# Block-transposed tiles sent from SBUF to SBUF in four transfers, in place of a way through DRAM

## The chip, the core and the metric

The kernel runs on one core of a Trainium2 chip. What counts is the time of one execution in microseconds (us) on the device. Five engines work side by side: PE multiplies matrices (PEld is its load of the stationary matrix), DVE, ACT and POOL work element by element, SP issues DMA transfers (ACT issues the stores). Each engine takes its instructions in the order of the program. On-chip data lies in SBUF, 128 partitions with a row each; PE writes to PSUM. A **stationary** operand of PE is loaded first (128 columns), the **moving** operand then streams past it, here 512 columns in a matmul.

## The reference

Queries of 4 batches, 8 heads, 768 positions and 64 features go in chunks of 32 positions. Each chunk sees 64 keys: 8 of a memory, 16 positions on the left, its own 32, and 8 on the right. The result goes through a mixture layer with two matrix products:

```python
scores = scale * np.matmul(q_c, k_full.transpose(0, 1, 3, 2))
scores = scores - np.max(scores, axis=-1, keepdims=True)
a = np.exp(scores)
a = a / (np.sum(a, axis=-1, keepdims=True) + 1e-09)
out[:, :, c_start:c_end] = np.matmul(a, v_full)
...
h = x @ w_in                                   # (3072, 512) @ (512, 1024)
e = np.exp(h - h_max)
sm = e / (np.sum(e, axis=-1, keepdims=True) + 1e-09)
solu = h * sm
ln = (solu - mu) / np.sqrt(var + 1e-06) * g_ln
return (ln @ w_out).astype(np.float32)         # (3072, 1024) @ (1024, 512)
```

## The kernel before

The 3072 rows are 24 tiles of 128. Attention works on **items**: items 0 and 1 are one tile each, items 2 to 12 two tiles each (item i holds tiles 2i-2 and 2i-1). The second part works on tiles 0 to 23. One text, ORDER, lists every step by name, in the order in which all engines get their instructions; it was planned ahead and is the same in both kernels. A name is a step and its item or tile, with the engine behind an @ (V is DVE, S is ACT, G is POOL).

For an item i the steps are: loads Lq, Lk, Lv (line 232); S, the scores on PE (line 347); M, the row maximum, and Bm, the subtraction of it (DVE, lines 370 and 377); X, the exponential (ACT, line 383); Z, the row sum (DVE, line 387); a transposition of the probabilities p; V, their product with the values (PE, line 415); N, the division by the row sum (DVE, line 429); a transposition of the result x; XH and XL, which split x into a rounded part and a rest (lines 216 or 214, and 219). For a tile t: G, 24 matmuls with w_in (line 480); Hm, He, Hu, C, Sq, Dn, the normalization; a transposition of u; UH and UL, the split; O, 24 matmuls with w_out (line 540); Os and St, the scaled store. Each of the two products is three matmuls in place of one, high by high, high by low, low by high.

A transposition is made in one of two ways. **On PE** (PT, XT, UT, line 333): items 0 to 3 and tiles 0 to 3. **By blocks** (Pt, Xt, Ut with Pw, Xw, Uw and Pr, Xr, Ur): the other 9 items, twice each (p and x), and the other 20 tiles, 38 tiles of data of 128 by 1024 in all. There DVE transposes each block of 32 by 32 in place (`square`, line 304), one transfer writes the tile to DRAM (`write`, line 312), and four transfers read it back into the same tile, each into 32 partitions (`read`, line 320):

```python
a = away[name, i].rearrange("(q n) (d e) -> q n d e", q=4, d=4)
for d in range(4):
    nc.sync.dma_start(t[SQ * d:SQ * d + SQ], a[:, :, d].rearrange("q n e -> n q e"))
```

All of these are issued by SP, in the place in ORDER of Pw and Pr (or Xw, Xr, Uw, Ur), between the loads of q, k and v. SP waits at a `read` until its `write` has landed, and what stands behind it on SP waits too. Transfers of SP and ACT count on eight semaphores in turn, so each also waits for the one eight places before it.

Tiles come from pools of buffers: `take` gives the buffer that has been free longest, and `used` gives one back after its last use.

Of the kernel before, what the change touches and what calls it, by code (L numbers as in the profile page):

```python
# [11 lines left out]
F32 = mybir.dt.float32  # L12
# [3 lines left out]
ALU = mybir.AluOpType  # L16
AX = mybir.AxisListType

P = 128
CHUNK, LEFT, RIGHT = 32, 16, 8  # L20
NEG = -1.0e30
SQ = 32
SLOTS, HALVES, RAWS, ROUNDED = 7, 6, 4, 8
SINGLES = 2
SPLIT = {0: 2}


# [2 lines left out]
ORDER = """  # L30
# [59 lines left out]
def chunked_attention_then_solu_kernel(  # L90
# [22 lines left out]
    nc = tc.nc  # L113
    D = P // 2
    NP_ = w_in.shape[0] // (2 * D)
    NT = out.shape[0] // P
    NCH = P // CHUNK
    LINE = kw.shape[0] // (NT * P * NP_)
    KEYS = P // 2
    DM, DF = w_in.shape  # L120
    items = [(t, 1) for t in range(SINGLES)] + [(t, 2) for t in range(SINGLES, NT, 2)]
    NC_ = DM // P
    NF = DF // P
    HALF = DF // 2
    TPB = 6
# [7 lines left out]
    dram = ctx.enter_context(tc.tile_pool(name="away", bufs=1, space=bass.MemoryType.DRAM))  # L133
# [5 lines left out]
    held = {}  # L139
    away = {}  # L140
# [12 lines left out]
    def get(*key):  # L153
        return held[key][0]

    def used(*key):
        held[key][1] -= 1
        if held[key][1] == 0:
            buf, _, kind = held.pop(key)
            if kind == "raw":  # L160
                rest[0] -= 1
                if rest[0] < RAWS:
                    free["slot"].extend([buf[:, 0:W], buf[:, W:2 * W]])
                    return
            free[kind].append(buf)
# [13 lines left out]
    w_in_h = const.tile([P, NC_, DF], F32R, name="w_in_h")  # L179
    w_in_l = const.tile([P, NC_, DF], F32R, name="w_in_l")  # L180
# [66 lines left out]
    def cut(ap, i, x):  # L247
        n = ap.shape[1] // SPLIT.get(i, 1)
        return ap[:, x * n:(x + 1) * n]
# [46 lines left out]
    def home(i):  # L296
        return "slot" if items[i][1] == 2 else "half"

    def square(name, item, uses):
        def step(i):  # L300
            src = get(name, i)
            kind = home(i) if item else "slot"
            t = take(kind, (name + "t", i), uses).rearrange("p (d m n) -> p d m n", d=4, n=SQ)
            nc.vector.transpose(t, src.rearrange("p (m d n) -> p d m n", d=4, n=SQ))  # L304
            used(name, i)
        return step

    def write(name):
        def step(i):
            t = get(name + "t", i)  # L310
            away[name, i] = dram.tile(list(t.shape), F32, name=f"{name}_away{i}")
            nc.sync.dma_start(away[name, i], t)
        return step

    def read(name):
        def step(i):
            t = get(name + "t", i).rearrange("p (q e) -> p q e", q=4)
            a = away[name, i].rearrange("(q n) (d e) -> q n d e", q=4, d=4)
            for d in range(4):
                nc.sync.dma_start(t[SQ * d:SQ * d + SQ], a[:, :, d].rearrange("q n e -> n q e"))  # L320
        return step

    def by_block(ap):
# [2 lines left out]
    def on_pe(name):  # L326
        def step(i):
            src = get(name, i)
            kind = "two" if name == "u" or items[i][1] == 2 else "one"
            t = take(kind, (name + "T", i), 1 if name == "p" else 2)  # L330
            t = flat(t) if kind == "two" else t
            for n in range(src.shape[1] // P):
                nc.tensor.transpose(t[:, n * P:(n + 1) * P], src[:, n * P:(n + 1) * P], ident)  # L333
            used(name, i)
        return step
# [20 lines left out]
    def by_head(i):  # L356
        n = items[i][1]
        return get("s", i)[:, :, 0:n * HALF // 2].rearrange("p r (n k) -> p r n k", k=KEYS)

    def row_max(i):  # L360
# [9 lines left out]
        nc.vector.tensor_reduce(nmax, s, axis=AX.X, op=ALU.max, negate=True)  # L370
        used("s", i)

    def below_max(i):
        n = items[i][1]
        nmax = get("nmax", i)[:, 0:2 * n * NP_].rearrange("p (r n) -> p r n", r=2).unsqueeze(3)
        a = take(home(i), ("p", i), 2).rearrange("p (n r k) -> p r n k", r=2, k=KEYS)
        nc.vector.tensor_tensor(a, by_head(i), nmax.broadcast_to([P, 2, n * NP_, KEYS]), ALU.add)
        used("s", i)
        used("nmax", i)

# [3 lines left out]

    def row_sum(i):
        s = take("per_head", ("rinv", i), 1)[:, 0:2 * items[i][1] * NP_]
        nc.vector.tensor_reduce(  # L387
            s, get("p", i).rearrange("p (n k) -> p n k", k=KEYS), axis=AX.X, op=ALU.add
        )
        nc.vector.tensor_scalar(s, s, 1e-9, None, ALU.add)  # L390
        nc.vector.reciprocal(s, s)
        used("p", i)
# [31 lines left out]
    def norm(i):  # L424
        n = items[i][1]
        rinv = get("rinv", i)[:, 0:2 * n * NP_].rearrange("p (n r) -> p r n", r=2).unsqueeze(3)
        x = take(home(i), ("x", i), 1).rearrange("p (n r d) -> p r n d", r=2, d=D)
        xp = get("xp", i)[:, :, 0:n * HALF // 2].rearrange("p r (n k) -> p r n k", k=D)
        nc.vector.tensor_tensor(x, xp, rinv.broadcast_to([P, 2, n * NP_, D]), ALU.mult)
        used("xp", i)  # L430
        used("rinv", i)

# [21 lines left out]
    def high(name, uses):  # L454
        def step(i, on):
            key, src = source(name, i)
            copy(on, target(name + "h", i, uses), src)
            used(*key)
        return step
# [9 lines left out]
    def hidden(t, c, half):  # L469
        if c == 0 and half == 0:  # L470
            take("two", ("h", t), 2)
        u, odd = divmod(t, 2)
        h = get("h", t)
        x = [
            get(n, u).rearrange("p (t c n) -> p t c n", t=2, n=P)[:, odd, c]
            for n in ("xh", "xl")
        ]
        w = (w_in_h, w_in_l)
        for i, (a, b) in enumerate(((0, 0), (0, 1), (1, 0))):
            nc.tensor.matmul(  # L480
                h[:, half], x[a], w[b][:, c, half * HALF:(half + 1) * HALF],
                start=c == 0 and i == 0, stop=c == NC_ - 1 and i == 2,
            )
        if c == NC_ - 1 and half == 1:
            used("xh", u)
            used("xl", u)
# [65 lines left out]
    def store(t):  # L552
# [24 lines left out]
def _layout(q, k, v, mem_k, mem_v):  # L577
    import numpy as np

    B, H, S, D = q.shape  # L580
    M = mem_k.shape[2]
    NPAIR = H // 2
    NCH = S // CHUNK
    KEYS = M + LEFT + CHUNK + RIGHT
    TPB = S // P
    CPT = P // CHUNK
    NT = B * TPB

    qT = q.reshape(B, NPAIR, 2, TPB, P, D).transpose(0, 3, 2, 5, 1, 4)
    qT = qT.reshape(NT, 2 * D, NPAIR, P)  # L590

    def padded(x):
        z = np.zeros((B, H, LEFT, D), x.dtype)
        return np.concatenate([z, x, z[:, :, :RIGHT]], 2)

    kp, vp = padded(k), padded(v)

    lines = []
    for t in range(TPB):
        x = kp[:, :, t * P:t * P + P + LEFT + RIGHT]  # L600
        mid = P - CHUNK
        lines.append(np.concatenate([x[:, :, :CHUNK], mem_k, x[:, :, CHUNK:mid], mem_k, x[:, :, mid:]], 2))
    kw = np.stack(lines, 1).reshape(B, TPB, NPAIR, 2, -1, D).transpose(0, 1, 3, 5, 2, 4)
    kw = kw.reshape(NT, 2 * D, NPAIR, -1)

    wins = []
    for c in range(NCH):
        x = vp[:, :, c * CHUNK:c * CHUNK + KEYS - M]
        e = 0 if c % 2 else CHUNK
        wins.append(np.concatenate([x[:, :, :e], mem_v, x[:, :, e:]], 2))  # L610
    vw = np.stack(wins, 2).reshape(B, NPAIR, 2, TPB, CPT, KEYS, D).transpose(0, 3, 2, 5, 1, 4, 6)
    vw = vw.reshape(NT, 2 * KEYS, NPAIR, CPT, D)
    def by_item(x):
        n = x.shape[0]
        late = x[SINGLES:].reshape((n - SINGLES) // 2, 2, P, -1).transpose(0, 2, 1, 3)
        return np.concatenate([x[:SINGLES].ravel(), late.ravel()])

    return by_item(qT), by_item(kw), by_item(vw)
# [28 lines left out]
```

## Time and profile before

| | |
|---|---|
| time, median of 3 runs (lowest to highest) | 359.84 us (356.36 to 359.94) |
| profiled execution: its time, its span | 359.48 us, 357.7 us |
| busy share of PE, DVE, POOL, ACT | 91%, 61%, 39%, 36% |
| mean granted clock of PE | 0.97 |
| chain that ended last, by engine | PE 61%, DMA 18%, DVE 12%, SP's queue 3%, ACT 3% |
| bytes moved by DMA | 82.31 MB, 230 GB/s on average |
| read from DRAM, written to DRAM | 55.45 MB, 26.21 MB |

The span runs from the first instruction to the last; all stretches below are counted in us from its start. "Busy" of PE is modelled, as matmuls overlap; how far apart they start says more. [...] The chain follows the last instruction back to what released it, step by step. A wait is put down to what ended it.

### The profile page before, as it was taken

The numbers are of one execution on the slowest core, as the hardware profiler recorded it, in microseconds if no ns is written. First come the engines' busy times: TensorE is split into PE (matmuls) and PEld (weight loads), VectorE is DVE, ScalarE is ACT, GpSimd is POOL, SyncE is SP. The second block draws the span as 40 slices with busy tenths as digits, with TensorE's granted clock in tenths as the row PEclk, the third lists the DMA queues.
The fourth block names the chain that finished last, engine by engine and source line by source line (L and its number), as shares of the span: only waits on it lengthen the run. The fifth ranks groups of instructions, "written<-read, shape, count | busy, mean of one in ns | idle before, by whom it ended". The sixth has DMA issues, their size and how long they took to land.

```text
span 357.7 us, 9973 instructions
## 1 busy us (share of the span) xinstructions
PE 325.8 (91%) x4324; PEld 263.7 (74%) x4324; DVE 219.7 (61%) x264; ACT 130.0 (36%) x189; POOL 138.9 (39%) x173
## 2 busy tenths in 40 slices
PE   1569999999997999979999899999959999999995
PEld 1557887888785877857887678888647888888884
DVE  1589999968966964756955386564466654037300
ACT  3256375542422414122322334422225064232521
POOL 0226061442318263752500834220523746625160
PEclk9969999999998999998999999999969999999999
DMA  7999925576897876689959679866651547435621
GB/s 296 420 422 400 405 78 199 198 252 192 302 306 218 245 267 214 220 233 353 268 191 263 194 216 382 286 188 188 212 210 60 184 114 226 128 129 173 226 90 59
DMA packets 37771, 82.31 MB, mean 230 GB/s; under 512 B 4320, under 2 KB 23776, under 8 KB 35296
## 3 DMA queue, kind: packets, MB, share of 16 engines
q1 hardware_dynamic: 34272, 75.39, 62.8%
q10 hardware_dynamic: 3456, 6.29, 4.7%
q8 instruction: 34, 0.56, 0.6%
q14 instruction: 9, 0.07, 0.1%
HBM read 55.45 MB, written 26.21 MB: 228 GB/s over the span
## 4 chain that ended last, share of the span: by engine, by line
PE 61%; DMA 18%; DVE 12%; SPq 3%; ACT 3%; issue 2%; POOL 1%; DVEq 0%; POOLq 0%; ACTq 0%
PE one L540 28%; PE two L480 23%; DMA out<-half 5%; PE two L347 4%; PE two L415 3%; SPq L320 3%; DMA q<-in_qT 2%; DMA raw<-p_away 2%; DMA k<-in_kw 2%; DVE per_head L387 2%; DMA p_away<-raw 2%; DMA raw<-x_away 1%; DMA slot<-x_away 1%; PE two L203 1%; PE two L333 1%
## 5 line engine op out<-in xcount | busy, mean ns | idle before, releaser
L480 PE MATMUL two<-w_in_h,fr 128*128 128x512 f32 x384 | 143.0, 405 | 6.8 <-DVE fr L219 4.6
L540 PE MATMUL one<-w_out_h,fr 128*128 128x512 f32 x384 | 138.1, 396 | 0.1
L480 PEld LDWEIGHTS two<-w_in_h,fr 128*128 128x128 f32 x384 | 73.4, 192 | 26.1 <-DVE fr L219 5.4
L540 PEld LDWEIGHTS one<-w_out_h,fr 128*128 128x128 f32 x384 | 72.7, 189 | 16.8 <-DVE fr L219 0.5
L480 PE MATMUL two<-w_in_l,fr 128*128 128x512 f32 x192 | 76.2, 397 | 0.2 <-DVE w_in_l L219 0.2
L540 PE MATMUL one<-w_out_l,fr 128*128 128x512 f32 x192 | 75.2, 391 | 0.0
L489 DVE TENSOR_REDUCE per_row<-two 128x1 f32<-128x1024 f32 x24 | 29.1, 1212 | 28.9 <-PE two L480 28.8
L548 ACT ACTIVATE half<-one,per_row 128x512 f32<-128x512 f32 x24 | 16.5, 687 | 82.2 <-PE one L540 80.8
L480 PEld LDWEIGHTS two<-w_in_l,fr 128*128 128x128 f32 x192 | 36.9, 192 | 7.7 <-DVE w_in_l L219 0.6
L540 PEld LDWEIGHTS one<-w_out_l,fr 128*128 128x128 f32 x192 | 36.5, 190 | 7.3
L219 POOL TENSOR_TENSOR fr<-raw,fr 128x1024 fp32r<-128x1024 f32 x13 | 31.2, 2403 | 17.4 <-ACT fr L214 16.6
L347 PE MATMUL two<-k,q 64*32 64x64 f32 x1536 | 19.6, 237 | 14.5 <-DMA k<-in_kw 7.6
L347 PEld LDWEIGHTS two<-k,q 64*32 64x32 f32 x1536 | 17.1, 111 | 18.8 <-issue 17.9
L216 POOL TENSOR_SCALAR fr<-raw 128x1024 fp32r<-128x1024 f32 x11 | 11.6, 1051 | 47.1 <-DVE slot L304 18.1
L219 POOL TENSOR_TENSOR fr<-slot,fr 128x1024 fp32r<-128x1024 f32 x9 | 21.5, 2391 | 18.1 <-DMA slot<-u_away 10.7
L494 ACT ACTIVATE slot<-two,per_row 128x1024 f32<-128x1024 f32 x12 | 13.4, 1118 | 30.6 <-DVE per_row L489 30.6
L494 ACT ACTIVATE raw<-two,per_row 128x1024 f32<-128x1024 f32 x12 | 13.4, 1115 | 27.7 <-DVE per_row L489 21.4
L216 POOL TENSOR_SCALAR fr<-slot 128x1024 fp32r<-128x1024 f32 x8 | 8.4, 1052 | 32.4 <-DMA slot<-u_away 15.3
L504 DVE CUSTOM_DVE_ANT_0 slot<-two,slot 128x1024 f32<-128x1024 f32 x12 | 14.7, 1222 | 8.1 <-ACT slot L494 8.1
L504 DVE CUSTOM_DVE_ANT_0 raw<-two,raw 128x1024 f32<-128x1024 f32 x12 | 14.5, 1206 | 7.7 <-ACT raw L494 6.2
L370 DVE TENSOR_REDUCE per_head<-two 128x16 f32<-128x1024 f32 (+1 forms) x13 | 14.8, 1135 | 5.0 <-PE two L347 4.7
L304 DVE STREAM_TRANSPOSE raw<-slot 128x1024 f32<-128x1024 f32 x10 | 12.4, 1238 | 8.1 <-POOL slot L516 5.9
(88 smaller groups left out, 372.9 us busy)
## 6 DMA issues: line engine op xcount, KB each, us to landing
v<-in_vw SPq DMA_DIRECT2D x11, 1024.0 KB, 8.5
k<-in_kw SPq DMA_DIRECT2D x11, 672.0 KB, 6.8
out<-half ACTq DMA_DIRECT2D x24, 256.0 KB, 3.0
u_away<-raw SPq DMA_DIRECT2D x12, 512.0 KB, 3.5
raw<-u_away SPq DMA_DIRECT2D x48, 128.0 KB, 3.4
q<-in_qT SPq DMA_DIRECT2D x11, 512.0 KB, 7.8
raw<-in_w_in SPq DMA_DIRECT2D x4, 1024.0 KB, 11.3
raw<-in_w_out SPq DMA_DIRECT2D x4, 1024.0 KB, 9.2
```

What stands on the lines that cost most here:

```text
L216: nc.gpsimd.tensor_scalar(out, in_, 1.0, 0.0, ALU.mult, ALU.add)
L219: (nc.gpsimd if on == "G" else nc.vector).tensor_tensor(out, a, b, ALU.subtract)
L304: nc.vector.transpose(t, src.rearrange("p (m d n) -> p d m n", d=4, n=SQ))
L320: nc.sync.dma_start(t[SQ * d:SQ * d + SQ], a[:, :, d].rearrange("q n e -> n q e"))
L347: nc.tensor.matmul(s[32 * j:32 * j + 32, r, t, g], q[rows, o + t, g, 32 * j:32 * j + 32], k[rows, o + t, g, START[j]:START[j] + KEYS], sta ...
L370: nc.vector.tensor_reduce(nmax, s, axis=AX.X, op=ALU.max, negate=True)
L480: nc.tensor.matmul(h[:, half], x[a], w[b][:, c, half * HALF:(half + 1) * HALF], start=c == 0 and i == 0, stop=c == NC_ - 1 and i == 2,)
L489: nc.vector.tensor_reduce(take("per_row", ("hm", t), 1), flat(get("h", t)), axis=AX.X, op=ALU.max, negate=True)
L494: nc.scalar.activation(take("slot", ("u", t), 2), flat(get("h", t)), AF.Exp, bias=get("hm", t), scale=1.0, accum_out=take("per_row", ("esu ...
L504: nc.vector.tensor_tensor_reduce(u, flat(get("h", t)), u, 1.0, 0.0, ALU.mult, ALU.add, accum_out=usum)
L540: nc.tensor.matmul(get("o", t), u[a], w[b][:, f], start=f == 0 and i == 0, stop=f == NF - 1 and i == 2)
L548: nc.scalar.mul(take("half", ("osb", t), 1), get("o", t), get("rstd", t))
```

## The change

The step `write` now takes a second buffer and sends the tile into it directly, in four transfers, each from 32 source partitions to all 128; `read` does nothing. By this the data land in another order: feature n of block d comes to partition 4n+d, where it was 32d+n. Everything that is multiplied with such a tile has to be in the same order. The host permutes rows and columns of w_in, and the values of tiles 6 and later. Items whose p goes by blocks get their p written by DVE in groups of 16 (`below_max`), two instructions in place of one, and their row sum is taken in two instructions. Items whose x goes through PE (0 to 3) get x written in the new order in `norm`, two instructions with a step of 4 elements. Tiles 0 to 3, whose u goes through PE, need the hidden columns in the old order: their G matmuls read w_in with a step of 32 elements (128 bytes).

```diff
@@ def write(name)
         def step(i):
-            t = get(name + "t", i)
-            away[name, i] = dram.tile(list(t.shape), F32, name=f"{name}_away{i}")
-            nc.sync.dma_start(away[name, i], t)
+            src = get(name + "t", i)
+            kind = home(i) if name != "u" else "slot"
+            uses = held[name + "t", i][1]
+            held[name + "s", i] = held.pop((name + "t", i))
+            t = take(kind, (name + "t", i), uses)
+            held[name + "s", i][1] = 1
+            src = src if len(src.shape) == 2 else flat(src)
+            e = src.shape[1] // 4
+            for q in (0, 2, 1, 3):
+                nc.sync.dma_start(t[:, e * q:e * q + e], src[SQ * q:SQ * q + SQ])
+            used(name + "s", i)
@@ def read(name)
-            t = get(name + "t", i).rearrange("p (q e) -> p q e", q=4)
-            a = away[name, i].rearrange("(q n) (d e) -> q n d e", q=4, d=4)
-            for d in range(4):
-                nc.sync.dma_start(t[SQ * d:SQ * d + SQ], a[:, :, d].rearrange("q n e -> n q e"))
+            pass
@@ def below_max(i)
+        a = take(home(i), ("p", i), 2)
+        if f"PT{i}" in todo:
...
+        else:
+            a = a.rearrange("p (n d r m) -> p r n d m", d=4, r=2, m=KEYS // 4)
+            for r in range(2):
+                nc.vector.tensor_tensor(
+                    a[:, r], by_head(i)[:, r].rearrange("p n (d m) -> p n d m", d=4),
+                    nmax[:, r].unsqueeze(3).broadcast_to([P, n * NP_, 4, KEYS // 4]), ALU.add,
+                )
@@ def row_sum(i)
+            a = get("p", i).rearrange("p (n d r m) -> p r n d m", d=4, r=2, m=KEYS // 4)
+            for r in range(2):
+                nc.vector.tensor_reduce(
+                    s.rearrange("p (n r) -> p r n", r=2)[:, r], a[:, r], axis=AX.XY, op=ALU.add
+                )
@@ def norm(i)
+        if f"XT{i}" in todo:
+            x = x.rearrange("p (n m r a) -> p r n a m", m=SQ, r=2, a=2)
+            for r in range(2):
+                nc.vector.tensor_tensor(
+                    x[:, r], xp[:, r].rearrange("p n (a m) -> p n a m", a=2),
+                    rinv[:, r].unsqueeze(3).broadcast_to([P, n * NP_, 2, SQ]), ALU.mult,
+                )
@@ def hidden(t, c, half)
-        w = (w_in_h, w_in_l)
+        w = [m[:, c, half * HALF:(half + 1) * HALF] for m in (w_in_h, w_in_l)]
+        if f"UT{t}" in todo:
+            w = [m.rearrange("p (f d n) -> p f n d", d=4, n=SQ) for m in w]
@@ on the host
+    place = np.arange(KEYS)
+    place = KEYS // 4 * (place % 4) + place // 4
+    vw = vw.reshape(NT, 2, KEYS, NPAIR, CPT, D)
+    vw = np.concatenate([vw[:AHEAD], vw[AHEAD:, :, place]])
...
+    there, here = 4 * (block % SQ) + block // SQ, SQ * (block % 4) + block // 4
+    hidden = np.arange(DF).reshape(-1, P, 2).transpose(0, 2, 1)
+    column = hidden[:, :, there].ravel()
+    row = np.arange(H * D).reshape(-1, P)[:, here].ravel()
```

How the order of instructions moves is seen at two places. On SP, around the last load of q for item 10 (q_94 from in_qT), this stood before; p_away is the probabilities of item 8, u_away and x_away are tiles of u and x:

```order
L320 DMA slot_65<-u_away_1715 32x4x256 x4
L320 DMA raw_78<-x_away_1876 32x4x256 x4
L312 DMA p_away_2061<-slot_63 128x1024
L320 DMA slot_63<-p_away_2061 32x4x256 x4
L232 DMA k_96<-in_kw 128x1344
L232 DMA q_94<-in_qT 128x1024
```

and this stands there now:

```order
L320 DMA slot_66<-raw_79 128x1x256 x4
L233 DMA v_98<-in_vw 128x2048
L320 DMA slot_67<-slot_68 128x1x256 x4
L233 DMA k_96<-in_kw 128x1344
L233 DMA q_94<-in_qT 128x1024
L320 DMA raw_76<-raw_78 128x1x256 x4
```

The load of q stood behind a write of p and the reads that wait for it; it now stands behind four transfers that wait for nothing of their own making.

On DVE, at the row sum and the block transposition of item 4's probabilities and the steps around it, before (raw_78 is p of item 4, slot_67 that of item 5):

```order
L377 TENSOR_TENSOR raw_78<-two_88,per_head_107 128x2x8x64
L304 STREAM_TRANSPOSE raw_78<-raw_78 128x1024
L377 TENSOR_TENSOR slot_67<-two_89,per_head_108 128x2x8x64
L304 STREAM_TRANSPOSE slot_63<-slot_67 128x1024
L387 TENSOR_REDUCE per_head_109<-raw_78 128x16
```

and now:

```order
L391 TENSOR_TENSOR raw_78<-two_88,per_head_107 128x32x16 x2
L305 STREAM_TRANSPOSE raw_78<-raw_78 128x1024
L391 TENSOR_TENSOR slot_67<-two_89,per_head_108 128x32x16 x2
L305 STREAM_TRANSPOSE slot_65<-slot_67 128x1024
L409 TENSOR_REDUCE per_head_109<-raw_78 128x8 x2
```

Subtraction and row sum are each in two halves; nothing else moved.

## Rows read from the trace of the kernel before

**Rows 1.** Timeline of PE: start, us, instruction, count, [idle before <- what ended it].
```profile
111.86 0.27 PE L415 MATMUL two<-v,raw 64*32 64x64 f32 x2 [1.42 <-DMA raw<-p_away]
112.97 1.52 PE L415 MATMUL two<-v,raw 64*32 64x64 f32 x126 [0.84 <-DMA raw<-p_away]
...
161.83 1.92 PE L347 MATMUL two<-k,q 64*32 64x64 f32 x128 [3.29 <-DMA q<-in_qT]
...
192.15 1.46 PE L415 MATMUL two<-v,slot 64*32 64x64 f32 x126 [0.71 <-DMA slot<-p_away]
199.80 0.50 PE L480 MATMUL two<-w_in_h,fr 128*128 128x512 f32 x1 [1.44 <-POOL fr L219]
...
262.91 1.22 PE L480 MATMUL two<-w_in_h,fr 128*128 128x512 f32 x2 [4.12 <-DVE fr L219]
```

**Rows 2.** Windows: stretch, length, busy of each engine (x instructions), clock, DMA share, GB/s.
```profile
36.00:110.00 74.00, 73.63 (x1317) 59.93 (x1316) 65.27 (x78) 33.68 (x45) 24.55 (x27) 1.00 0.71 242
112.97:118.00 5.03, 5.03 (x135) 4.14 (x136) 3.47 (x3) 1.06 (x3) 2.97 (x8) 0.66 0.20 79
161.83:167.00 5.17, 5.17 (x139) 4.40 (x140) 3.07 (x6) 0.00 (x0) 0.00 (x0) 0.67 1.07 377
199.80:203.00 3.20, 3.20 (x14) 2.62 (x15) 2.12 (x2) 0.00 (x0) 2.66 (x7) 1.00 0.31 99
262.91:268.50 5.59, 5.59 (x14) 4.40 (x15) 2.46 (x4) 1.78 (x3) 0.00 (x0) 0.56 0.56 188
```

**Rows 3.** Chain that ended last, in order of time: start, us, what.
```profile
99.60 5.43 DMA p_away<-raw
...
106.48 6.35 DMA raw<-p_away
112.97 1.52 PE two L415 x86
...
325.87 28.07 PE one L540 x123
```

**Rows 4.** Timeline of SP, its issues: start, us until issued, instruction, count.
```profile
151.96 2.12 SPq L320 DMA_DIRECT2D slot<-p_away  x4
154.19 0.38 SPq L232 DMA_DIRECT2D k<-in_kw  x1
154.60 0.43 SPq L232 DMA_DIRECT2D q<-in_qT  x1
...
248.97 0.34 SPq L312 DMA_DIRECT2D x_away<-slot  x1
252.25 2.05 SPq L320 DMA_DIRECT2D slot<-x_away  x4
```

**Rows 5.** Timelines of ACT and DVE before the wait at 262.91, columns as in rows 1.
```profile
256.95 1.05 ACT L214 CAST fr<-slot 128x1024 fp32r<-128x1024 f32 x1 [11.62 <-DMA slot<-x_away]
257.90 1.05 ACT L383 ACTIVATE raw<-raw 128x1024 f32<-128x1024 f32 x1
...
258.99 1.25 DVE L304 STREAM_TRANSPOSE raw<-raw 128x1024 f32<-128x1024 f32 x1 [3.01 <-ACT raw L383]
260.16 2.69 DVE L219 TENSOR_TENSOR fr<-slot,fr 128x1024 fp32r<-128x1024 f32 x1
```

**Rows 6.** DMA issues: tiles, queue, count, KB each, median us from issue to landing.
```profile
x_away<-raw SPq DMA_DIRECT2D x4, 512.0 KB, 6.4
slot<-p_away SPq DMA_DIRECT2D x16, 128.0 KB, 2.9
```

**Rows 7.** Groups by form: line, instruction, count | busy us, mean ns | idle before.
```profile
L377 DVE TENSOR_TENSOR slot<-two,per_head 128x1024 f32<-128x1024 f32 x5 | 6.1, 1223 | 0.2
...
L383 ACT ACTIVATE half<-half 128x512 f32<-128x512 f32 x2 | 1.3, 631 | 6.8 <-DVE half L377 6.8
...
L273 DVE SCALAR_TENSOR_TENSOR slot<-raw,slot 128x512 uint32<-128x512 uint32 x2 | 1.4, 682 | 0.0
L377 DVE TENSOR_TENSOR half<-two,per_head 128x512 f32<-128x512 f32 x2 | 1.4, 687 | 0.0
L260 ACT ACTIVATE slot<-raw 128x512 f32<-128x512 f32 x2 | 1.2, 660 | 3.6 <-DMA raw<-in_w_in 3.6
```

**Rows 8.** Timeline of PE at a granted clock of 0.56.
```profile
264.35 1.05 PE L480 MATMUL two<-w_in_h,fr 128*128 128x512 f32 x2
265.21 0.63 PE L480 MATMUL two<-w_in_l,fr 128*128 128x512 f32 x1
```

More of the change, by code (lines that the diff above doesn't have):

```diff
@@ L24 @@
 SINGLES = 2
+AHEAD = 6
 SPLIT = {0: 2}
@@ L371, in row_max @@
         used("s", i)
+    todo = set(ORDER.split())
     def below_max(i):
@@ L375, in below_max @@
         nmax = get("nmax", i)[:, 0:2 * n * NP_].rearrange("p (r n) -> p r n", r=2).unsqueeze(3)
-        a = take(home(i), ("p", i), 2).rearrange("p (n r k) -> p r n k", r=2, k=KEYS)
-        nc.vector.tensor_tensor(a, by_head(i), nmax.broadcast_to([P, 2, n * NP_, KEYS]), ALU.add)
+        a = take(home(i), ("p", i), 2)
+        if f"PT{i}" in todo:
+            a = a.rearrange("p (n r k) -> p r n k", r=2, k=KEYS)
+            nc.vector.tensor_tensor(a, by_head(i), nmax.broadcast_to([P, 2, n * NP_, KEYS]), ALU.add)
+        else:
[5 more added lines that the diff above has]
+                )
         used("s", i)
@@ L386, in row_sum @@
         s = take("per_head", ("rinv", i), 1)[:, 0:2 * items[i][1] * NP_]
-        nc.vector.tensor_reduce(
-            s, get("p", i).rearrange("p (n k) -> p n k", k=KEYS), axis=AX.X, op=ALU.add
-        )
+        if f"PT{i}" in todo:
+            nc.vector.tensor_reduce(s, get("p", i).rearrange("p (n k) -> p n k", k=KEYS), axis=AX.X, op=ALU.add)
+        else:
+            a = get("p", i).rearrange("p (n d r m) -> p r n d m", d=4, r=2, m=KEYS // 4)
[3 more added lines that the diff above has]
+                )
         nc.vector.tensor_scalar(s, s, 1e-9, None, ALU.add)
@@ L426, in norm @@
         rinv = get("rinv", i)[:, 0:2 * n * NP_].rearrange("p (n r) -> p r n", r=2).unsqueeze(3)
-        x = take(home(i), ("x", i), 1).rearrange("p (n r d) -> p r n d", r=2, d=D)
         xp = get("xp", i)[:, :, 0:n * HALF // 2].rearrange("p r (n k) -> p r n k", k=D)
-        nc.vector.tensor_tensor(x, xp, rinv.broadcast_to([P, 2, n * NP_, D]), ALU.mult)
+        x = take(home(i), ("x", i), 1)
+        if f"XT{i}" in todo:
[5 more added lines that the diff above has]
+                )
+        else:
+            x = x.rearrange("p (n r d) -> p r n d", r=2, d=D)
+            nc.vector.tensor_tensor(x, xp, rinv.broadcast_to([P, 2, n * NP_, D]), ALU.mult)
         used("xp", i)
@@ L477, in hidden @@
         ]
-        w = (w_in_h, w_in_l)
+        w = [m[:, c, half * HALF:(half + 1) * HALF] for m in (w_in_h, w_in_l)]
+        if f"UT{t}" in todo:
+            w = [m.rearrange("p (f d n) -> p f n d", d=4, n=SQ) for m in w]
         for i, (a, b) in enumerate(((0, 0), (0, 1), (1, 0))):
             nc.tensor.matmul(
-                h[:, half], x[a], w[b][:, c, half * HALF:(half + 1) * HALF],
+                h[:, half], x[a], w[b],
                 start=c == 0 and i == 0, stop=c == NC_ - 1 and i == 2,
@@ L610, in _layout @@
         wins.append(np.concatenate([x[:, :, :e], mem_v, x[:, :, e:]], 2))
-    vw = np.stack(wins, 2).reshape(B, NPAIR, 2, TPB, CPT, KEYS, D).transpose(0, 3, 2, 5, 1, 4, 6)
+    wins = np.stack(wins, 2)
+    vw = wins.reshape(B, NPAIR, 2, TPB, CPT, KEYS, D).transpose(0, 3, 2, 5, 1, 4, 6)
+    place = np.arange(KEYS)
+    place = KEYS // 4 * (place % 4) + place // 4
+    vw = vw.reshape(NT, 2, KEYS, NPAIR, CPT, D)
+    vw = np.concatenate([vw[:AHEAD], vw[AHEAD:, :, place]])
     vw = vw.reshape(NT, 2 * KEYS, NPAIR, CPT, D)
@@ L628 @@
     DF = moe_g_ln.shape[0]
-    column = np.arange(DF).reshape(-1, P, 2).transpose(0, 2, 1).ravel()
-    g = moe_g_ln[column].reshape(-1, P).T
-    w_in, w_out = (np.ascontiguousarray(w).view(np.uint64) for w in (moe_w_in[:, column], moe_w_out))
+    block = np.arange(P)
+    there, here = 4 * (block % SQ) + block // SQ, SQ * (block % 4) + block // 4
+    hidden = np.arange(DF).reshape(-1, P, 2).transpose(0, 2, 1)
+    column = hidden[:, :, there].ravel()
+    row = np.arange(H * D).reshape(-1, P)[:, here].ravel()
+    g = moe_g_ln[hidden.ravel()].reshape(-1, P).T
+    w_in, w_out = (np.ascontiguousarray(w).view(np.uint64) for w in (moe_w_in[row][:, column], moe_w_out))
     ins = dict(zip(_INS, (qT, kw, vw, w_in, w_out, g)))
```

## The prediction

> **What bounds the kernel now.** I read the waits of PE first, then the windows, then the chain of waits, then SP's queue, and last the groups by form. PE is busy for 91% of the span. From 36 to 110 us it works without a break (73.63 of 74.00 us at a granted clock of 1.00, the first of [rows 2]), and from 326 us to the end it does nothing but matmuls with w_out, 123 of them in 28.07 us, 0.228 us each [rows 3]. So any time that is added to PE's instructions is added to the kernel, and the only time to be won lies in PE's waits. After the start there are five of note [rows 1]: at 112.97 for p of item 6 (1.42 + 0.84), at 161.83 for a load of q (3.29), at 192.15 for p of item 10 (0.71), at 199.80 for POOL's split of x of item 8 (1.44), at 262.91 for DVE's split of x of item 11 (4.12). Together 11.82 us. Behind three of them PE runs at a lower clock: 0.66 for 5.03 us, 0.67 for 5.17 us, 0.56 for 5.59 us, which costs 1.71 + 1.71 + 2.46 = 5.88 us; behind the wait of 1.44 us the clock stays at 1.00 [rows 2]. All five come from the way through DRAM, as the next part shows, so **17.7 us** is the most that the change can give back here. The start (before 36 us) has no such transfer and keeps its length.
>
> **What is removed, wait by wait.** Each of the 38 tiles had a write and four reads one behind the other. For p of item 6 the write is issued at 99.60, lands after 5.43, the last of its reads takes 6.35, and PE uses it at 112.97 [rows 3]: 13.4 us. Now the four transfers go out at once. The trace has no transfer from SBUF to SBUF, so I bound it by the four reads' issue (2.12 us, [rows 4]) plus a landing between the shortest and the longest median of these transfers, 2.9 and 6.4 us [rows 6]: 5.0 to 8.5 us, of which I take 5.5, since one new transfer has the bytes and the piece size (1 KB) of one read. The pieces, 1 KB each and 128 to a transfer, are the same in both.
> - *112.97*: data at 104.6 to 108.1 instead of 112.97. PE wants it at 110.4. Gone at either end.
> - *161.83*: the load of q is issued at 154.60, because SP first waited for the write of p of item 8 to land (the reads start at 151.96) and issued the reads [rows 4]. The landing of that write, at least 2.9 us, drops out ahead of the load. Gone or down to 0.4, and too short to touch the clock.
> - *192.15 and 199.80*: 0.71 and 1.44 us against a saving of 4.9 us or more per tile (13.4 less 8.5). Gone.
> - *262.91*: the write of x of item 11 goes out at 248.97, its reads at 252.25 [rows 4], and ACT's rounding starts at 256.95 after 11.62 us of waiting; behind it on ACT stands the exponential of item 12 (257.90), behind that on DVE the block transposition (258.99), and behind that the split that PE waits for (260.16, 2.69 us) [rows 5]. With data 8.0 us after the issue now and 5.5 then, the line moves up by 2.5 us. That leaves 1.6 us of the 4.12, again too short for the clock by the row at 199.80.
>
> Buffers: a tile now holds two buffers from the issue until the transfer has landed. The pools hand out the buffer that was free longest, and at each new `take` at least three others are free in the program's order, so what is late next is no buffer but DVE's and ACT's own work. I leave 1.6 us at 262.91 and 0.9 us for waits that show up elsewhere: **gain 17.7 - 2.5 = 15.2 us**.
>
> **What is added.** *SP*: 38 writes fewer, 152 transfers as before; each stands where the write stood, so loads behind the old reads come earlier. Nothing on the path. Where a store stands eight places ahead, a transfer still waits for it, as now. *DVE*: 22 instructions more (9 subtractions, 9 row sums, 4 divisions in halves). Two halves of 128x512 take 2 x 687 against 1223 ns [rows 7], 0.15 us more each, 3.3 us in all on an engine that is 61% busy. The stretch where PE waits on DVE's results in turn is the start: three of the divided steps (N of items 0 to 2) lie before 36 us, where DVE is the engine that everything waits for: **+0.5 us**. The rest has cover, since DVE's chain for p and x becomes shorter by 5 us or more of transfer; without that cover it would cost at most the 3.3.
>
> *PE*: the 96 G matmuls of tiles 0 to 3 (4 x 24) read w_in with a step of 128 bytes. They all run between 32 and 85 us, where PE has no slack, so their cost counts in full. No row of this trace shows a moving operand with a step. [...] The nearest rows are other engines that read SBUF with a step of 8 bytes [rows 7]: DVE takes 682 ns with it and 687 without, ACT 660 with and 631 without, 5% more. The farthest is the same matmul at half clock, 0.86 us for two, 0.43 each [rows 8]: 96 x (0.43 - 0.228) = 19.4 us. I take the dearer of the near rows and raise it to 8%, because the step is longer: 96 x 0.228 x 0.08 = **+1.7 us**.
>
> [...]
>
> **Sum** against the profiled execution's 359.5 us (0.4 below the median of 359.84): 359.5 - 15.2 + 0.5 + 1.7 = **346.5 us**. Its own range, with 2 to 6 us of waits left and 0 to 4 us for the step, is 343 to 351.
>
> **Rivals.**
> - *A. The stepped read halves PE's rate* (other side). Mechanism: for 96 matmuls PE gets one column for two of its clocks. For it: PE takes in 512 columns in 0.228 us, 2.2 columns in the time in which DVE reads one (512 in some 0.53 us, 687 ns less a start of 0.15), so PE stands closer to what the memory gives than the engines of [rows 7] do. Against it: those engines lose at most 5% to a step. Price 19.4 us: 359.5 - 15.2 + 0.5 + 19.4 = 364.2; the slower start gives the waits that are left time to vanish, down to 361.7. Range 358 to 367, slower than before in more than half of it. [...] It decides from 0.153 us a matmul on (14.7 / 96), that is at 0.38 us or 1.7 times the time.
> - *B. The new transfers are slow.* Each reads from 32 partitions only and lands near 8.5 us, with loads beside it (DMA share 1.07 in one of [rows 2]). Then the wait at 262.91 stays whole with its clock (4.12 + 2.46), as its data came after 8.0 us already, and half of the one at 161.83 (2.5): 346.5 + 5 to 9 = 351 to 357, say 354.
> - *C. A and B together, or a step that costs more than half the rate*: above 367.
> - *D. The change doesn't do what it says*: the waits come back one for one behind stores that stand eight places ahead on the semaphores, or behind ACT and DVE. Against it: the rows of SP show the old waits at the reads themselves. 358 to 361.
>
> **Chances.** Forecast 0.44, A 0.36, B 0.10, C 0.06, D 0.04. A measurement of this kernel tells about 1% (3.6 us) from no change. Faster than 356.2: forecast 0.44 and most of B, 0.08: 0.52. Between 356.2 and 363.4: the lower part of A 0.16, D 0.04, the rest of B 0.02: 0.22. Above: the upper part of A 0.20 and C 0.06: 0.26. The range has to reach from the forecast through A, as these hold 0.8 of the chance: 343 to 367.
>
> **What would show it.** In the profile of the changed kernel: G matmuls of tiles 0 to 3 should start 0.23 to 0.25 us apart between 32 and 85 us; 0.38 or more means A. PE's waits for p, for q and behind the splits of x should be gone or under 1.5 us, and the clock 1.00 from 36 to 325 us, where now three stretches lie at 0.56 to 0.67. From issue to landing the new transfers should take 2.9 to 4 us; 6 or more is B. Bytes from and to DRAM should fall by 19.9 MB each (38 x 0.524). PE should begin its last run of matmuls with w_out some 13 us before 326. The prediction is wrong if the stepped matmuls are slow or the waits only move.

## The result, and the profile after

The changed kernel takes **346.47 us** (median of 4 runs, 345.05 to 346.62) against 359.81 us before (median of 4 runs on the same chip, 356.36 to 359.94). The ratio is 0.9642, 95% interval 0.958 to 0.9705: faster by 3.6%. Here and below a time is the median of all runs, and a ratio leaves out runs more than 1.5% above the fastest of their kernel. The forecast was 346.5 us. The total is right; the experiments show that the cause given for the gain is mostly wrong, and that two costs were missed or too small.

The waits of PE in the changed kernel (engine, tile and line, what ended the wait: us in total, times, longest):

```profile
PE two L353 <- DMA k<-in_kw: 7.6, 1, 7.6
PE one L339 <- ACT half L400: 3.2, 1, 3.2
PE two L353 <- issue: 2.3, 1, 2.3
PE two L437 <- issue: 2.2, 1, 2.2
PE one L339 <- DVE half L454: 0.2, 1, 0.2
```

The first three lie in the start, as they did before, and so does the last, which is new and short. All five waits of [rows 1] are gone. The fourth is new: PE stops in the middle of item 5's values without a wait for a semaphore that the profile shows ("issue"). The timeline of PE shows it, and shows the stepped matmuls (start, us, instruction, count):

```profile
45.27 0.71 PE L513 MATMUL two<-w_in_h,fr 128*128 128x512 f32 x2
45.81 0.44 PE L513 MATMUL two<-w_in_l,fr 128*128 128x512 f32 x1
46.08 0.71 PE L513 MATMUL two<-w_in_h,fr 128*128 128x512 f32 x2
...
95.39 1.07 PE L437 MATMUL two<-v,raw 64*32 64x64 f32 x60 [2.23 <-issue]
```

Three stepped matmuls take from 45.27 to 46.08, 0.27 us each, against 0.228 in [rows 3]. The windows, with the columns of [rows 2]:

```profile
95.00:100.00 5.00, 4.62 (x71) 3.75 (x71) 4.36 (x6) 0.00 (x1) 0.67 (x1) 0.66 0.04 11
100.00:115.00 15.00, 15.00 (x72) 12.49 (x71) 8.71 (x12) 4.61 (x7) 5.81 (x7) 1.00 0.69 223
115.00:310.00 195.00, 194.99 (x2305) 159.91 (x2304) 125.47 (x158) 69.56 (x106) 88.69 (x110) 1.00 0.54 151
```

From 100 to 310 us PE does not stop and its clock is 1.00. The one stretch at a lower clock (0.66 of full speed over 5 us, with 0.50 from 95.5 to 98.9) follows the new stop. The last run of matmuls with w_out, which began at 325.87 [rows 3], now begins 14.3 us earlier (chain of waits):

```profile
311.55 28.09 PE one L573 x123
```

The fastest and the slowest of the four kinds of new transfers (columns as in [rows 6]), and the new divisions on DVE (line, tiles, forms, count | busy us, mean ns | idle before):

```profile
raw<-slot SPq DMA_DIRECT2D x44, 128.0 KB, 2.6
...
raw<-raw SPq DMA_DIRECT2D x32, 128.0 KB, 3.5
```

```profile
L391 DVE TENSOR_TENSOR raw<-two,per_head 128x512 f32<-128x512 f32 x6 | 3.9, 686 | 0.1
...
L454 DVE TENSOR_TENSOR raw<-two,per_head 128x512 f32<-128x512 f32 x2 | 2.0, 1108 | 0.0
```

The transfers land after 2.6 to 3.5 us, where the forecast looked for 2.9 to 4. The subtractions cost 686 ns a half, as forecast; the divisions of 128x512 at the start, which write with a step of 16 bytes, cost up to 1108 ns where 687 was assumed.

Laying the two kernels' matmuls side by side by their number gives the account, for the two profiled executions (359.48 and 345.05 us). The changed kernel is 0.3 us ahead at 31 us, 2.0 behind at 87 (stepped matmuls), 5.3 behind at 104 (the new stop and the clock behind it), and 14.3 ahead at the end. From 104 us on it therefore wins 19.6 us: 4.9 by 149 us, where p of item 6 was waited for, 5.1 by 190 (the load of q), 1.8 by 206 (p of item 10 and POOL's split), 7.5 at the split of x of item 11, and 0.4 between. That is the list of [rows 1], with 1.9 us more than its waits and clocks came to.

### The profile page after: what moved, and what is told of

Its sections match the earlier page's. It is cut to its first block, busy times and chain, and to the rows that moved or that the text cites. A ratio compares the mean times of both kernels' runs of the same rounds, so it can differ in the third digit from the quotient of the medians.

```text
span 343.3 us, 9936 instructions
## 1 busy us (share of the span) xinstructions
PE 324.0 (94%) x4324; PEld 262.4 (76%) x4324; DVE 223.3 (65%) x286; ACT 130.2 (38%) x189; POOL 139.7 (41%) x173
## 4 chain that ended last, share of the span: by engine, by line
PE 94%; issue 2%; DMA 2%; DVE 1%; ACT 0%; SPq 0%
PE two L513 40%; PE one L573 39%; PE two L353 6%; PE two L437 5%; PE two L339 2%; DMA k<-in_kw 2%; PE two L204 1%; PE one L339 1%; DVE half L454 0%; DVE half L387 0%; DVE per_head L376 0%; ACT half L581 0%; ACT half L400 0%; SPq L233 0%; SPq L257 0%
## 5 line engine op out<-in xcount | busy, mean ns | idle before, releaser
L513 PE MATMUL two<-w_in_h,fr 128*128 128x512 f32 x384 | 141.3, 401 | 0.0
L513 PEld LDWEIGHTS two<-w_in_h,fr 128*128 128x128 f32 x384 | 72.3, 188 | 18.1
L513 PEld LDWEIGHTS two<-w_in_l,fr 128*128 128x128 f32 x192 | 36.1, 188 | 8.1
L527 ACT ACTIVATE raw<-two,per_row 128x1024 f32<-128x1024 f32 x15 | 16.8, 1118 | 35.1 <-DVE per_row L522 31.0
L537 DVE CUSTOM_DVE_ANT_0 raw<-two,raw 128x1024 f32<-128x1024 f32 x15 | 18.3, 1218 | 10.9 <-ACT raw L527 9.5
L217 POOL TENSOR_SCALAR fr<-slot 128x1024 fp32r<-128x1024 f32 x10 | 10.5, 1054 | 34.1 <-PE one L573 22.2
L562 POOL TENSOR_SCALAR per_row<-per_row,per_row 128x1 f32<-128x1 f32 x24 | 7.0, 292 | 39.7 <-ACT raw L554 29.9
L554 ACT ACTIVATE raw<-raw 128x1024 f32<-128x1024 f32 x15 | 15.7, 1049 | 9.0 <-DVE slot L305 9.0
L305 DVE STREAM_TRANSPOSE slot<-raw 128x1024 f32<-128x1024 f32 x12 | 14.8, 1237 | 4.1 <-ACT raw L547 2.6
L549 POOL TENSOR_SCALAR raw<-raw,per_row 128x1024 f32<-128x1024 f32 x6 | 6.8, 1126 | 26.2 <-DVE per_row L540 26.2
```

The costliest lines, as they stand in the source:

```text
L513: nc.tensor.matmul(h[:, half], x[a], w[b], start=c == 0 and i == 0, stop=c == NC_ - 1 and i == 2,)
L527: nc.scalar.activation(take("slot", ("u", t), 2), flat(get("h", t)), AF.Exp, bias=get("hm", t), scale=1.0, accum_out=take("per_row", ("esu ...
L537: nc.vector.tensor_tensor_reduce(u, flat(get("h", t)), u, 1.0, 0.0, ALU.mult, ALU.add, accum_out=usum)
L554: nc.scalar.activation(u, u, AF.Square, accum_out=take("per_row", ("var", t), 1))
```

## Experiments

Each ratio is to the kernel before, on the same chip in the same rounds. Of the twelve times, only those of traffic and new_reads fall into a range that was expected; the others are read by which waits came or went.

**1. Put the way through DRAM back (route_all).** The changed kernel with every other edit kept.

```
-  for q in (0, 2, 1, 3): dma(t[:, e*q:e*q+e], src[32q:32q+32])
+  write: dma(away, t)
+  read:  for q in (0, 2, 1, 3): dma(t[:, e*q:e*q+e], away[32q:32q+32])
```

> Changed kernel, but every tile goes through DRAM as before: a write at Pw, Xw, Uw, four reads at Pr, Xr, Ur into the same buffer, in the new order of features. All other edits stay. Theory (the gain is the time from write to data, and what stands behind the reads on SP): the waits of before come back, and the stepped matmuls cost 96 x 0.046 us on top: 361 to 366 us. Rival (the gain comes from the other edits: buffers, halves on DVE, the new order): it stays at 347 to 352 us.

Measured: **342.80 us**, ratio 0.9618 (0.9563 to 0.9672). The waits of PE and the DMA row of the page (queue: packets, MB, share of the 16 engines):

```profile
PE two L363 <- DMA k<-in_kw: 7.3, 1, 7.3
PE one L349 <- ACT half L410: 3.2, 1, 3.2
PE two L363 <- issue: 2.9, 1, 2.9
PE two L447 <- issue: 1.5, 1, 1.5
```

```profile
q1 hardware_dynamic: 34272, 75.39, 62.8%
```

The bytes and packets are those of the kernel before, and all five waits are gone all the same. So leaving out DRAM was not needed to remove them; the theory of the prediction fell here. The time, 342.80, lies below the ranges of both theories.

**2. Parts of the way through DRAM, and idle traffic (route_u, route_px, traffic).** As in 1, for u alone or for p and x alone; and the changed kernel with one write more per tile that nobody reads.

```
+  VIA = "u"      (route_u)       VIA = "px"     (route_px)
+  dma(copy, src)  after the four transfers of a tile   (traffic)
```

> Changed kernel, but the 20 tiles of u go through DRAM, p and x directly. Theory: PE's five waits of before were for p, for x and for a load behind p, so few come back: 347 to 352 us. Rival (any read that waits on SP holds up all that stands behind it, whoever's it is): 20 of 38 tiles bring back at least half of the 13 us, 353 to 360 us.

> Changed kernel, but the 18 tiles of p and x go through DRAM, u directly. Theory: the waits for p and x come back, 357 to 364 us, with PE waiting at the values of items 6 and 10 and behind the split of x of items 8 and 11. Rival (the waits go by the number of tiles on SP): about half comes back, 352 to 354 us.

> Changed kernel with one write of each tile to DRAM added behind its four transfers (38 x 0.52 MB, total bytes back to 82 MB); nobody reads it, only the reuse of the source buffer waits for it. Theory (time from write to data): 346 to 349 us. Rival (the gain is the 20 MB that DRAM and the DMA engines no longer carry, which let loads and transfers land sooner): more than half of the 13 us is given back, 354 to 360 us.

Measured: route_u 345.82 us, ratio 0.9713 (0.9663 to 0.9764); route_px 347.28, 0.975 (0.9681 to 0.9819); traffic 348.43, 0.9783 (0.972 to 0.9846). All three keep most of the gain, in line with 1; the intervals of the last two reach past 0.98, so that they are faster by 2% is not certain. None of the waits that were expected to come back in route_px did. The 38 writes more of traffic go through SP's queue too, so its time is a bound for bytes and queue together: about 5 us (0.014 of 357) more than the changed kernel, and the two intervals just miss each other. In its profiled execution PE's stops without a semaphore alone are 3.7 us longer (8.2 us in all against 4.5).

**3. The reads' shape alone, and all but the reads' shape (new_reads, old_reads).** What is left between route_all and the kernel before is the shape of the four reads and the edits on PE, DVE and the inputs. Two runs complete the square.

```
 new_reads: the kernel before, with
-  dma(t[32d:32d+32], away of block d, "q n e -> n q e")    d in 0..3
+  dma(t[:, e*q:e*q+e], away[32q:32q+32])                   q in 0, 2, 1, 3
 old_reads: route_all with the opposite edit
```

> The kernel before with the reads' shape alone changed: four transfers, each from 32 rows into all 128 partitions; the features then lie in another order than weights and values have, no other edit is made. Theory 'shape': the five old waits go without any other edit, and TensorE has no stepped operands: 338 to 344 us. Theory 'slack': TensorE is as early as before and waits as before: 355 to 360 us.

> All edits of the change but the way of the tiles: through DRAM, and read back in the old shape (four transfers, each into 32 partitions, old feature order, so the weights' and values' order no longer fits). It differs from the run through DRAM that took 342.8 us in the reads' shape alone. Theory 'shape' (reads into 32 partitions land 128 KB in 0.55 to 0.6 us, p6: 111.01, 111.72, 112.28, 112.83; reads into 128 partitions in 0.33 us, 111.62, 111.94, 112.28, 112.61, and that took the old waits away): the waits of TensorE for transposed tiles and for q10 come back, 355 to 362 us. Theory 'slack' (TensorE is some 2 us later by 54 us because of the stepped matmuls, and so finds its data there): the reads' shape does nothing, 341 to 345 us.

Measured: new_reads **341.48 us**, ratio 0.9591 (0.9523 to 0.966); old_reads **363.27 us**, 1.0207 (1.0136 to 1.0278). The square:

| | other edits of before | other edits of the change |
|---|---|---|
| old reads | 357.0 (1) | 363.3 (1.021) |
| new reads | 341.5 (0.959) | 342.8 (0.962) |
| no DRAM | not run | 346.5 (0.964) |

Among the kernels that go through DRAM the reads' shape carries the whole gain. With the old shape the other edits cost 6.3 us, and PE waits as before:

```profile
PE two L363 <- DMA q<-in_qT: 5.1, 1, 5.1
PE two L523 <- DVE fr L221: 4.0, 1, 4.0
...
PE two L447 <- DMA raw<-p_away: 2.3, 2, 1.6
PE two L447 <- DMA slot<-p_away: 1.5, 1, 1.5
```

The theory "slack" does not hold. What the shape does shows in two places. First, reads land sooner. The DMA issues from 95 us to the use of p of item 6, in the kernel before and in new_reads (columns as in [rows 6]):

```profile
slot<-x_away SPq DMA_DIRECT2D x4, 128.0 KB, 5.6
q<-in_qT SPq DMA_DIRECT2D x1, 512.0 KB, 7.8
raw<-p_away SPq DMA_DIRECT2D x4, 128.0 KB, 6.3
```

```profile
slot<-x_away SPq DMA_DIRECT2D x4, 128.0 KB, 4.8
q<-in_qT SPq DMA_DIRECT2D x1, 512.0 KB, 5.4
raw<-p_away SPq DMA_DIRECT2D x4, 128.0 KB, 3.9
```

By the landing times of the whole trace, a read that queues behind others (one that takes about 4 us or more from issue to landing) lands 0.55 us after its neighbour when it goes into 32 partitions (median of 35) and 0.34 us when it goes into 128 (median of 33): 238 and 386 GB/s. The load of q queued among them gains 2.4 us too. The reads of p are what the first wait of [rows 1] was for.

Second, SP no longer stands behind stores. The rows of SP's waits at the reads that name a store, of the kernel before, old_reads and new_reads, in this order (waiting line, what ended it: us, times, longest):

```profile
SPq L320 <- DMA out<-half: 31.5, 8, 6.5
```

```profile
SPq L336 <- DMA out<-half: 28.8, 7, 6.4
```

```profile
SPq L320 <- DMA out<-half: 0.5, 1, 0.5
```

In route_all and in the changed kernel there is no such row at the transposing transfers at all. In the kernel before, the chain of waits runs through these stores on its way to three of the five waits of PE (start, us, what):

```profile
140.48 6.84 DMA out<-half
147.34 0.30 SPq L320
...
148.69 3.26 DMA p_away<-slot
...
154.60 7.09 DMA q<-in_qT
...
161.83 0.21 PE two L347
...
187.45 3.13 DMA out<-half
190.60 5.31 DMA raw<-x_away
197.38 2.37 POOL fr L219
...
243.55 5.36 DMA out<-half
248.97 3.14 DMA x_away<-slot
```

The store of 140.48 has nothing to do with the tiles. It is read this way: the 262 transfers of this program share eight semaphores, which are handed out in turn when the kernel is built, and one that is to use a semaphore waits until the transfer that used it last has landed. In the trace the store issued at 140.48 and x's read issued at 147.34 carry the same one, number 109, and the read goes out 0.02 us after the store has landed. While SP waits there, all that stands behind on its queue waits too, the write of p at 148.69, its reads, and then the load of q. With the reads in the new shape the stores carry other semaphores, ones that no read needs soon. The numbers in the traces show why this matters: by its number the store's turn comes behind 84 transfers of SP, but ACT gets to it only when SP has issued 89, so x's read, eight places behind it in turn, comes soon after it and waits. In new_reads both queues issue the same transfers in the same order, yet the store's turn comes behind 91, and SP has issued 90 when ACT gets to it.

**4. What makes the old shape slow (wide_read, narrow_block).** Two kernels that take the shape apart: into all partitions with pieces 4 KB apart, and into 32 partitions out of one block.

```
 wide_read:    dma(t[:, e*q:e*q+e], away[32q:32q+32] as "n (d e) -> d n e")
 narrow_block: dma(t[32d:32d+32] as "p (q e)", away[32d:32d+32] as 128 pieces, "(q n) e -> n q e")
```

> The kernel before with one edit that keeps its layout, weights and values as they are: tile through DRAM, read back in four transfers of 32 rows each, whose 1 KB pieces are taken in the order block, row, so that each transfer fills all 128 partitions and every feature lands where it did before. Theory 'destination' (a read is slow because it goes into 32 partitions): as fast as the run with the new reads alone (341.5 us), 339 to 344 us, neighbouring reads that are queued land 0.34 us apart, the five old waits gone. Theory 'source' (the old read was slow because its 1 KB pieces lie 4 KB apart in DRAM, the new one's follow each other): nothing gained, 355 to 360 us, 0.55 us apart, since here neighbouring pieces lie 4 KB apart again.

> The kernel before with reads that go into 32 partitions each as before, but whose source is one block of 128 KB in DRAM (32 whole rows, its 1 KB pieces in another order, so the features come to other places than the weights have). Theory 'destination': no gain, 355 to 360 us, 0.55 us apart. Theory 'source': 339 to 345 us, 0.34 us apart.

Measured: wide_read **441.35 us**, ratio 1.2306 (1.2257 to 1.2356); narrow_block 353.51 us, 0.9883 (0.9825 to 0.9941), its queued reads 0.55 us apart (median of 31). The time of narrow_block lies between the two theories, but its reads are as slow as the old ones, so the source is not what makes the old read slow, as "destination" said. The other half of that theory met something that neither had foreseen. wide_read's page has, for the same bytes:

```profile
q1 hardware_dynamic: 32448, 75.38, 47.4%
```

That is 1824 packets fewer than the 34272 of the kernel before, all of them under 512 B (2496 on the page, 4320 before): 12 for each of the 152 reads. The trace of the kernel before has 4193 packets of 4 bytes, 16 for each of its 262 transfers and one more, so a read of wide_read is left with 4. In a stretch with nothing but such reads (window of wide_read):

```profile
110.25:111.00 0.75, 0.75 (x4) 0.56 (x4) 0.00 (x0) 0.00 (x0) 0.00 (x0) 0.89 0.27 97
```

The DMA share is 0.27 there and the rate 97 GB/s. Of 16 engines that is the time of 4.3, so by an estimate from the share and the packets about 4 of them worked. The slowest dimension of such a read is the 4 blocks; that it sets this number was not shown, as no other number was tried.

**5. The same reads in another order, and the reordering on the write (alternate, four_one).**

```
 alternate: -  for d in range(4)          (reads of the kernel before)
            +  for d in (0, 2, 1, 3)
 four_one:  four writes in 1 KB pieces that put the tile into DRAM in its final order,
            dma(away[q] as "(d n) e -> n d e", t[32q:32q+32]), then one read of 512 KB
```

> The kernel before with the four reads of a tile issued in the order of blocks 0, 2, 1, 3 instead of 0, 1, 2, 3; nothing else is changed, each read still goes into 32 partitions. [...] Theory 'count': 32 partitions are slow in any order: 355 to 360 us, 0.55 us apart.

> The kernel before with its layout, weights and values kept, through DRAM with the reordering on the other side: four writes, each of 32 partitions in 1 KB pieces, in the order 0, 2, 1, 3, put the tile into DRAM in its final order, and one read of 512 KB fills all 128 partitions. [...] Theory 'reads': the reads' shape was all that held the kernel, 339 to 345 us, the five old waits gone, no stepped matmuls. Rival: four writes from 32 partitions each are now as slow as the reads were, and the reads wait for them: 350 to 358 us.

Measured: alternate 353.82 us, ratio 0.9888 (0.9824 to 0.9952); four_one **361.61 us**, 1.0194 (1.0132 to 1.0255). In alternate queued reads land 0.47 us apart (median of 35) instead of the 0.55 that "count" expected, and the time falls by 1.1% to just under that theory's range, which is as much as narrow_block gained at 0.55. SP itself issues the reads of a tile 0.475 us apart (median, kernel before), so the issue may set a part of the 0.47. So the order of the blocks does little for the time, and reads that are faster by this much do not bring the 4%. What the kernels with a time near the old one have in common is the waits of SP, here of alternate, narrow_block and four_one:

```profile
SPq L320 <- DMA out<-half: 28.4, 7, 5.7
```

```profile
SPq L320 <- DMA out<-half: 30.3, 8, 7.7
```

```profile
SPq L314 <- DMA out<-half: 32.9, 6, 9.7
```

With before and old_reads these are five kernels with 28 to 33 us of such waits, and they took 353 to 363 us; the eight that took 341 to 349 us have at most 0.5 us. In alternate, narrow_block and old_reads the store of experiment 3 has its turn behind 84 transfers of SP, as before. wide_read stands apart: its turns are those of new_reads (behind 91), it has no such wait at all, and it is slow by its reads.

four_one shows the effect of a single wait. The five old waits are gone or at most 1.1 us and its small writes land after 3.1 to 4.0 us, so neither theory's reason holds. But one of its writes stands behind a store, SP is stuck for 9.7 us, and the chain of waits goes from there to a new wait of PE of 7.0 us. PE's stops without a semaphore are longer too, 9.9 us in all against 3.6 before, which adds 6.3 us more. The kernel before took 358.13 us in the same rounds, at the median of 17 runs, so a loss is not certain. The chain:

```profile
222.53 2.02 DMA out<-half
224.56 0.30 SPq L314
...
227.36 6.79 DMA v<-in_vw
234.16 6.14 DMA slot<-u_away
240.35 0.65 PE two L418 x28
```

**6. The price of the stepped matmuls (nostep).**

```
-  if f"UT{t}" in todo: w = [m.rearrange("p (f d n) -> p f n d", d=4, n=SQ) for m in w]
```

> The changed kernel with the moving operand of the first matmuls of tiles 0 to 3 contiguous (their hidden features then come in another order than w_out has). Theory 'price': 96 matmuls at 0.228 instead of 0.273 us give 96 x 0.046 = 4.4 us back: 341 to 343 us. Theory 'slack': TensorE comes 4 us earlier to its operands and waits for them again: 344.5 to 347 us, with waits for transposed tiles in the trace.

Measured: 343.24 us, ratio 0.9608 (0.9552 to 0.9664); against 0.9642 for the changed kernel the intervals overlap, so the time settles nothing between 0 and 4 us. In the trace the matmuls are 0.227 us apart again and no wait for a block-transposed tile comes back, so "slack" does not hold here either. By the matmuls' numbers the profiled execution, which at 346.93 us is the longest of the four (the others took 341.45 to 343.97), gains 2.6 us between 26 and 62 us and gives 2.1 of them back in the stop of item 5's values, which lasts 3.3 us there with a clock of 0.50 behind it, where the changed kernel has 2.2 us and 0.66. That stop need not be as long in the other three.

**7. The new stop (loads).** Two loads later in the written order.

```
-  ... O3.7 Lv7 G7.0.0 G6.0.0 / Lq8 Xt5 G7.0.1 G6.0.1 St0 Xw5 G7.1.0 ...
+  ... O3.7 G7.0.0 G6.0.0 / Xt5 G7.0.1 G6.0.1 St0 Xw5 Lv7 Lq8 G7.1.0 ...
```

> The changed kernel with two loads (v7 and q8) moved in the order behind x5's transposition, so that fewer bytes are queued at 88 to 92 us. Theory: the stop of TensorE in the middle of V5 (1.07 us shown with the wait 'issue' of 2.2, then a granted clock of 0.66 in 95 to 100 us) is its program's fetch (one 16 KB packet of the instruction queue at 93.06 us) behind those loads: it goes, with the lower clock behind it, 342 to 344 us. Rival: the stop is not the loads' and stays, 346 to 347 us.

Measured: 345.55 us, ratio 0.9684 (0.9637 to 0.9731), no different from the changed kernel. The stop and the low clock are gone (window of loads, to be held against 0.66 above):

```profile
95.00:100.00 5.00, 4.95 (x74) 3.78 (x57) 4.72 (x6) 3.29 (x4) 2.42 (x2) 1.00 0.16 56
```

PE now waits at 115.2 us for a transposed tile instead, 1.5 us in two pieces, and a longer stop of the same kind at 17.8 us (3.4 us, 2.3 in the changed kernel) takes the rest. So this stop hangs on the place of the two loads, and taking it away alone is worth nothing that was measured; the time lies between the two ranges that were expected. That PE's program is what arrives late behind them, one packet of 16 KB at 93.06 us, fits but is inferred: with the loads moved it came at 92.26.

## Why the prediction came out right

- **"All five come from the way through DRAM": wrong, the step that failed.** All five went, as forecast, but they also go with DRAM in the way (route_all, new_reads), and with the old reads they stay whatever else is edited (old_reads). At the load of q the prediction began with the write of p at 148.69 and did not ask why that came so late. [Rows 4] start at 151.96; the chain of waits that was quoted for p of item 6 has the answer a few lines on, the store at 140.48. Of the 17.7 us, 13.7 (3.29 + 1.71 at q, 0.71, 1.44, 4.12 + 2.46) lie, by the trace, behind times in which SP stood behind a store, and 4.0 (1.42 + 0.84 + 1.71 at p of item 6) behind slow reads into 32 partitions. The chain passes a store on the way to all of the first sum but the 0.71, ahead of which SP stands too, for a store at 183.5.
- **"Where a store stands eight places ahead, a transfer still waits for it, as now": this sentence held the real cause and put it at nothing.** Which store stands eight places ahead is settled when the kernel is built, and the edit of the reads moved it (from behind 84 of SP's transfers to behind 91). Rival D had stores that hold up transfers as a danger of the change; they were what the kernel before suffered from.
- **2.5 us left over: too much.** Nothing was left at 262.91, and PE won back 19.6 us where 17.7 was called the most. The times of rivals B and D did not come: the transfers land after 2.6 to 3.5 us and no old wait is left.
- **0.5 us for DVE: its total is right, its parts are not.** DVE is busy 223.3 us against 219.7, 3.6 us more where 3.3 was forecast, though the divisions cost 1108 ns a half where 687 was assumed. At the end of the start the changed kernel is 0.3 us ahead, with the stop at 17 us shorter by 1.3 (2.3 against 3.6), so about 1 us went there.
- **1.7 us for the stepped matmuls: too small.** 0.273 us against 0.228, 20% and not 8%: 96 x 0.046 = 4.4 us. Of that 2.4 show in the time by 87 us, and 0.9 stand where the kernel before had three short waits (0.44, 0.19 and 0.24 us); the rest is not accounted for. The near rows were no price of a step: DVE's 687 ns is for an instruction that reads PSUM, its 682 for another that reads SBUF. Rival A needed 0.38 us and is out. A step of 128 bytes is worth 1.20 times here, not twice.
- **The new stop: not foreseen.** 3.3 us between 87 and 104 us, with a clock of 0.66 where the prediction looked for 1.00 from 36 to 325 us.

So 19.6 won from 104 us on and 5.3 lost before it make 14.3, where the prediction had 15.2 won and 2.2 lost, 13.0: errors of 4.4 and 3.1 us that leave 1.3. Those are the profiled executions, and the changed kernel's was the shortest of its four (345.05 us, median 346.47), which hides the rest. That the forecast met the median to 0.1 us is luck.

**What stays open.** In new_reads faster reads and other turns of the semaphores came together. alternate has somewhat faster reads with the old turns, and wide_read the new turns with far slower reads, so neither prices one of the two alone, and the split of 4.0 and 13.7 is read from the trace, not measured by itself. Why the build gives the stores an earlier turn when the reads go into 32 partitions was not tried. A direct way in the old shape, four transfers into 32 partitions each, was not run, so whether leaving out DRAM alone would have removed the waits is open too. Of the direct transfers themselves the runs show no gain: the ratio is 0.9642 without DRAM and 0.9618 with it, 19.9 MB less each way notwithstanding. No kernel that was run is clearly faster than the changed one. PE's stops without a semaphore add up to between 2.7 us (old_reads) and 9.9 us (four_one); differences of a few us between kernels can be theirs.

## What to carry to other kernels

A wait for a transfer is followed back to what held the queue that issued it, not to the transfer: look at SP's own waits, and if a store or a load that has nothing to do with the tile ends them, it is a shared semaphore and any edit to the transfers may move it. Before a change of layout is credited, its parts are to be tried one at a time: here the shape of four reads was worth as much as the whole change. Two transfers of the same bytes can differ much in cost: a queued read took 1.6 times as long into 32 partitions as into 128, and wide_read's reads, taken in 4 blocks, ran at 97 GB/s.

## What the runs showed of the hardware that was not expected

- The same 128 KB, queued, takes 0.55 us into 32 partitions and 0.34 into 128, and 0.47 when neighbouring reads go to blocks 0, 2, 1, 3. Why 32 partitions take 1.6 times as long was not shown; SP issues the reads of a tile 0.475 us apart, close to the third number.
- Reads of 128 KB taken in 4 blocks (wide_read) ran at 97 GB/s with a DMA share of 0.27, and the kernel took 23% longer.
- A matmul whose moving operand steps by 128 bytes starts 0.273 us after the one before, 1.20 times the contiguous one.
- DVE writing 128x512 with a step of 16 bytes (the divisions) takes 1069 to 1108 ns; the subtractions of the same size, which write runs, take 686.
- The eight semaphores, shared in turn, tie a transfer to the one eight places ahead, even one on another engine's queue: SP stood 31.5 us behind ACT's stores in the kernel before, 0.5 us in new_reads.
